# Attention with split fp16 operands in every unit, queries and keys packed on 128 partitions, and weight remainders formed on three engines

## The chip, the cores and the metric

One core of one Trainium2 chip runs the kernel. The time is the device time of one execution in microseconds (us). TensorE multiplies (the page calls it PE), VectorE (DVE) and ScalarE (ACT) work elementwise, GpSimd (POOL) does casts and reductions across partitions, and SyncE (SP) issues the DMAs.

## What is computed

Banded attention with block summaries, followed by a two-layer GELU network on its output. In the reference, cut to what matters:

```python
# q, k, v: (4, 8, 768, 64) fp32; blocks of 32 keys; window 16
k_sum = k.reshape(B, H, nb, 32, D).max(axis=3)
v_sum = v.reshape(B, H, nb, 32, D).mean(axis=3)
scores_l = scale * q @ k.T, masked to |i - j| < 16
scores_s = scale * einsum('bhsd,bhnd->bhsn', q, k_sum) + log(32)
a = softmax(concatenate([scores_l, scores_s], axis=-1))
x = (a @ concatenate([v, v_sum], axis=2)).transpose(0, 2, 1, 3).reshape(3072, 512)
h = x @ w_in                      # 512 x 2048
g = 0.5 * h * (1 + erf(h / sqrt(2)))
out = g @ w_out                   # 2048 x 512
```

w_in and w_out arrive as 64-bit floats.

## The kernel before

**Precision.** TensorE multiplies fp16. An fp32 value is carried as a high part, its fp16 rounding, and a low part, the fp16 rounding of what is left. A product then takes three fp16 matmuls: high by high, high by low, low by high.

**Units and chunks.** The work is cut into 12 chunks of 256 tokens. Attention goes in 24 units of four heads by 256 queries, two units to a chunk. A unit's steps, each a method of the class Unit with the unit's number, are: load_q, load_k, load_v and load_vs; k_hi and q_hi (casts on GpSimd); k_lo and q_lo (subtractions on VectorE); scores (TensorE, into the PSUM tile pss); add_mask (VectorE); maximum (an all-reduction over the partitions on GpSimd); shift (VectorE); exponent (ScalarE); p_hi (GpSimd) and p_lo (VectorE); v_hi (ScalarE) and v_lo (VectorE); values (TensorE); norm_den, norm_take, norm_rec, norm_spread and norm_mult (the division by the softmax sum, on ScalarE and VectorE); x_hi and x_lo.

In a unit from 4 on, k16 holds the high part of k on partitions 0 to 63 and the low part on 64 to 127, and q stands twice, on both halves. One matmul over 128 rows then gives high k by high q plus low k by high q, and a second adds the products with q's low part: 2 matmuls for each of 16 pairs of head and 64 queries.

Units 0 to 3 (self.fp, u < NF) take another way: scores and values multiply fp32 directly (scores_f, L576; values, L648), the mask is put into PSUM by an fp32 matmul (f_mask, L543), f_evac copies the scores out, and in units 0 and 1 the shift by the maximum is two more fp32 matmuls (f_shift, L551 and L552). Their k and v come from extra padded inputs kf and vf, which lie in parts of w_out_h and w_out_l that are not filled yet.

**The network.** phase1 c i (24 matmuls of 256 columns) makes 256 of the 2048 hidden values for chunk c; gelu, g_hi (ScalarE) and g_lo (VectorE) follow; phase2 c i (12 matmuls of 512 columns) multiplies by a quarter of w_out for half of the chunk's tokens. Step i of phase1 needs the weight pieces 2i and 2i + 1 of w_in.

**Weights.** w_in and w_out come in 16 pieces each of 128 x 512 numbers. wi_bits and wo_bits rebuild fp32 from the 64-bit words in three VectorE instructions in a buffer wst, of which there are three. wi_hi and wo_hi (ScalarE) make the scaled high part; wi_lo and wo_lo (VectorE, L324) the low part.

**Order.** ORDER is a long list of steps, written out; the program issues them in this order, and each engine runs its own instructions strictly in it, waiting at each for what it needs. The pools set what can run ahead: two PSUM tiles psh for phase1, one pss, one psv, three stage buffers for loads.

Of the kernel before, what the change touches and what calls it, by code (L numbers as in the profile page):

```python
# [67 lines left out]
norm_den 1, load_v 3, wi_bits 11 0, load_vs 2, shift 2, k_hi 4, scores 3, norm_take 1, exponent 2, load_q 4,
norm_rec 1, k_hi 5, norm_spread 1, norm_mult 1, load_vs 3, load_v 4, wi_bits 11 1, x_hi 1, values 2, wi_bits 11 2,
f_evac 3, q_hi 4, x_lo 1, wi_hi 11, wi_bits 12 0, maximum 3, wi_lo 11, wi_bits 12 1, load_v 5, wi_bits 12 2,  # L70
phase1 0 0, norm_den 2, wi_bits 15 0, fetch_w_out 0, wi_bits 15 1, wi_bits 15 2, load_vs 4, wi_hi 12, norm_take 2,
wi_hi 15, fetch_w_out 6, phase1 0 1, norm_rec 2, gelu 0 0, norm_spread 2, load_vs 5, norm_mult 2, g_hi 0 0, wi_lo 12,
phase1 0 2, x_hi 2, g_lo 0 0, gelu 0 1, x_lo 2, g_hi 0 1, v_hi 4, wi_lo 15, phase1 0 3, shift 3, gelu 0 2, g_hi 0 2,
wi_bits 13 0, load_q 5, exponent 3, wi_bits 13 1, phase1 0 7, wo_bits 0 0, wo_bits 0 1, wi_bits 13 2, gelu 0 3,
wo_bits 6 0, fetch_w_out 10, wo_bits 6 1, values 3, wo_bits 6 2, wi_hi 13, g_hi 0 3, wi_lo 13, wo_hi 6, wo_bits 0 2,
v_hi 5, g_lo 0 2, fetch_w_out 1, fetch_w_out 2, wo_hi 0, g_lo 0 1, phase1 0 6, norm_den 3, wo_lo 6, wo_lo 0, gelu 0 7,
norm_take 3, g_hi 0 7, norm_rec 3, phase1 0 4, norm_spread 3, gelu 0 6, wo_bits 1 0, g_hi 0 6, norm_mult 3,
phase1 0 5, wo_bits 2 0, x_hi 3, wo_bits 1 1, x_lo 3, wo_bits 1 2, wo_bits 2 1, wo_hi 1, wo_bits 2 2, wo_lo 1,
wo_hi 2, g_lo 0 3, wo_lo 2, gelu 0 5, wo_bits 10 0, g_hi 0 5, g_lo 0 7, g_lo 0 5, gelu 0 4, g_lo 0 6, g_hi 0 4,
phase1 1 1, wo_bits 10 1, wo_bits 10 2, k_lo 4, wo_hi 10, fetch_w_out 3, fetch_w_out 4, fetch_w_out 11, wo_lo 10,  # L80
q_lo 4, load_k 6, phase1 1 2, gelu 1 1, g_lo 0 4, g_hi 1 1, wo_bits 3 0, wo_bits 3 1, wo_bits 3 2, phase1 1 3,
gelu 1 2, wo_bits 4 0, fetch_w_out 5, wo_hi 3, wo_bits 4 1, g_hi 1 2, wo_lo 3, wo_bits 4 2, phase1 1 0, gelu 1 3,
# [5 lines left out]
fetch_w_out 14, phase2 0 3, wo_bits 12 0, wo_hi 8, fetch_w_out 15, wo_lo 9, wo_lo 8, g_lo 1 3, phase2 0 5,
wo_bits 12 1, wo_bits 12 2, wo_bits 14 0, wo_hi 12, fetch_k 1 1, wo_bits 14 1, phase2 0 4, wo_bits 15 0, wo_bits 15 1,
wo_bits 14 2, wo_bits 15 2, wo_hi 14, fetch_k 1 2, wo_lo 12, wo_hi 15, fetch_k 1 0, wo_lo 14, wo_lo 15, add_mask 4,  # L90
phase2 0 7, g_lo 1 2, maximum 4, k_lo 6, gelu 1 5, g_hi 1 5, phase2 0 6, gelu 1 4, k_lo 5, g_hi 1 4, store 0 1,
g_lo 1 4, load_k 7, phase1 1 7, put 0 1, shift 4, q_lo 5, exponent 4, load_q 6, phase1 1 6, g_lo 1 5, load_k 8,
v_lo 4, gelu 1 7, p_hi 4, prep_k 1 1, load_v 6, scores 5, p_lo 4, fetch_k 1 3, gelu 1 6, q_hi 6, g_hi 1 6, add_mask 5,
values 4, g_hi 1 7, k_hi 7, store 0 0, g_lo 1 7, put 0 0, phase2 1 1, norm_den 4, maximum 5, q_lo 6, norm_take 4,
prep_k 1 0, phase2 1 3, g_lo 1 6, shift 5, phase2 1 5, v_lo 5, exponent 5, load_q 7, k_lo 7, load_v 7, phase2 1 0,
p_hi 5, prep_k_end 1 0, load_k 9, norm_rec 4, k_sums 1 0, p_lo 5, phase2 1 2, norm_spread 4, norm_mult 4, prep_k 1 2,
x_hi 4, values 5, x_lo 4, fetch_v 1 0, fetch_v 1 1, prep_k 1 3, scores 6, norm_den 5, prep_k_end 1 1, fetch_v 1 3,
phase2 1 7, q_hi 7, add_mask 6, k_sums 1 1, k_hi 8, norm_take 5, phase2 1 4, maximum 6, store 1 1, norm_rec 5,
norm_spread 5, put 1 1, norm_mult 5, q_lo 7, phase2 1 6, x_hi 5, shift 6, x_lo 5, scores 7, exponent 6, load_q 8,
prep_v 1 0, phase1 2 2, store 1 0, k_hi 9, add_mask 7, put 1 0, fetch_v 1 2, p_hi 6, prep_v 1 1, phase1 2 1, gelu 2 2,  # L100
maximum 7, p_lo 6, fetch_k 2 2, k_lo 8, g_hi 2 2, phase1 2 0, gelu 2 1, g_lo 2 2, g_hi 2 1, load_k 10, q_hi 8,
prep_v 1 2, prep_v 1 3, phase1 2 3, gelu 2 0, g_hi 2 0, shift 7, load_vs 6, g_lo 2 0, phase1 2 4, exponent 7,
load_vs 7, q_lo 8, g_lo 2 1, load_q 9, gelu 2 3, p_hi 7, scores 8, fetch_k 2 3, k_lo 9, fetch_k 2 1, phase2 2 1,
k_hi 10, p_lo 7, v_hi 6, load_k 11, v_hi 7, v_lo 6, phase2 2 0, q_hi 9, gelu 2 4, v_lo 7, load_v 8, g_hi 2 4,
g_hi 2 3, add_mask 8, values 6, g_lo 2 3, maximum 8, q_lo 9, phase1 2 6, norm_den 6, load_vs 8, g_lo 2 4, norm_take 6,
norm_rec 6, load_v 9, norm_spread 6, phase1 2 5, gelu 2 6, norm_mult 6, g_hi 2 6, shift 8, v_hi 8, values 7, x_hi 6,
g_lo 2 6, load_q 10, exponent 8, load_vs 9, phase2 2 3, x_lo 6, v_lo 8, k_lo 10, norm_den 7, load_v 10, p_hi 8,
phase2 2 2, gelu 2 5, prep_k 2 3, load_k 12, norm_take 7, norm_rec 7, phase1 2 7, v_hi 9, norm_spread 7, norm_mult 7,
load_vs 10, g_hi 2 5, g_lo 2 5, x_hi 7, scores 9, p_lo 8, gelu 2 7, g_hi 2 7, phase2 2 4, q_hi 10, x_lo 7, k_hi 11,
add_mask 9, v_lo 9, phase1 3 0, maximum 9, g_lo 2 7, load_v 11, q_lo 10, phase1 3 2, gelu 3 0, k_lo 11, g_hi 3 0,  # L110
shift 9, load_k 13, phase1 3 5, gelu 3 2, load_vs 11, g_hi 3 2, g_lo 3 0, exponent 9, g_lo 3 2, load_q 11, prep_k 2 1,
# [742 lines left out]
```

## Time and profile before

| | |
|---|---|
| three runs | 683.58 us median (680.51 to 684.58) |
| the profiled execution | 686.86 us, its span 684.8 us |
| mean granted clock of TensorE | 0.945 |
| busy PE / DVE / ACT / POOL | 638.6 / 472.6 / 297.0 / 172.7 us |
| moved by DMA | 72.24 MB |

A row of a group reads: line, engine, operation, output<-inputs, shapes, count | busy us, mean ns of one | idle time before it and what ended it. A row of the timeline reads: start us, length us, engine, line, operation. A wait reads: who waits <- for whom: us in total, times, the longest.

### The profile page before, as it was taken

How to read it: one execution, taken by the hardware profiler on the slowest of the kernel's cores; microseconds unless marked ns; L12 is line 12 of the kernel's file. 1: busy time of each engine (PE TensorE's matmuls, PEld its weight loads, DVE VectorE, ACT ScalarE, POOL GpSimd, SP SyncE). 2: the span in 40 equal slices, each digit the busy share in tenths (PEclk: the TensorE clock that was granted, in tenths of full speed). 3: DMA queues.
4: the chain of work that ended last, by engine and by line, in shares of the span. 5: the costliest groups of instructions: out<-in, count | busy, mean ns of one | idle time of the engine just before them, and what ended most of it. 6: DMA issues, size and time to landing. Idle time of an engine off the chain costs nothing.

```text
span 684.8 us, 12436 instructions
## 1 busy us (share of the span) xinstructions
PE 638.6 (93%) x5356; PEld 444.2 (65%) x5356; DVE 472.6 (69%) x581; ACT 297.0 (43%) x419; POOL 172.7 (25%) x103
## 2 busy tenths in 40 slices
PE   1989999889898799999899989999999899999997
...
DVE  1784778999999998948889986628318974146210
...
PEclk9855569999999999999999999999999999999999
...
GB/s 247 378 218 199 139 66 125 149 180 152 162 117 141 167 91 225 180 57 72 91 127 79 88 77 53 133 1 111 45 16 66 84 69 16 1 32 1 16 16 32
DMA packets 26998, 72.24 MB, mean 105 GB/s; under 512 B 3008, under 2 KB 6720, under 8 KB 26944
## 3 DMA queue, kind: packets, MB, share of 16 engines
...
q8 instruction: 42, 0.69, 0.4%
...
HBM read 63.38 MB, written 6.29 MB: 102 GB/s over the span
## 4 chain that ended last, share of the span: by engine, by line
PE 66%; DVE 25%; issue 3%; DMA 2%; ACT 2%; POOL 1%; SPq 1%; DVEq 0%; ACTq 0%; POOLq 0%
PE psh L708 9%; PE psh L709 9%; PE psh L710 9%; PE pso L743 8%; PE pso L742 8%; PE pso L744 8%; PE psv L648 4%; DVE ql L568 3%; DVE gl L728 3%; PE pss L576 3%; DVE k L562 2%; DVE s L607 2%; DVE s L593 2%; PE pss L543 2%; DVE v_lo L634 2%
## 5 line engine op out<-in xcount | busy, mean ns | idle before, releaser
L708 PE MATMUL psh<-xh,w_in_h 128*128 128x256 f16 x768 | 210.4, 274 | 6.4 <-ACT g L715 6.4
L709 PE MATMUL psh<-xl,w_in_h 128*128 128x256 f16 x768 | 210.3, 274 | 0.5 <-DVE xl L698 0.5
L710 PE MATMUL psh<-xh,w_in_l 128*128 128x256 f16 x768 | 210.4, 274 | 0.0
L728 DVE SCALAR_TENSOR_TENSOR gl<-g,gh 128x512 f16<-128x512 f32 x96 | 76.7, 804 | 106.9 <-ACT gh L724 106.3
L743 PE MATMUL pso<-w_out_l,gh 128*128 128x512 f16 x384 | 146.4, 381 | 0.5 <-DVE w_out_l L324 0.5
L742 PE MATMUL pso<-w_out_h,gh 128*128 128x512 f16 x384 | 146.5, 382 | 0.0
L744 PE MATMUL pso<-w_out_h,gl 128*128 128x512 f16 x384 | 146.0, 380 | 0.0
L602 POOL PARTITION_ALL_REDUCE q<-s x24 | 82.5, 3439 | 95.9 <-ACT s L547 55.1
L715 ACT ACTIVATE g<-psh 128x512 f32<-128x512 f32 x96 | 56.9, 595 | 109.8 <-PE psh L710 107.9
L559 POOL CAST qh<-q 128x1024 f16<-128x1024 f32 x20 | 25.6, 1278 | 268.7 <-PE pss L589 254.7
L709 PEld LDWEIGHTS <-w_in_h 128*128 128x128 f16 x768 | 75.6, 98 | 18.8 <-issue 7.3
L708 PEld LDWEIGHTS <-w_in_h 128*128 128x128 f16 x768 | 75.7, 99 | 11.9
L710 PEld LDWEIGHTS <-w_in_l 128*128 128x128 f16 x768 | 75.5, 98 | 10.0 <-issue 0.9
L744 PEld LDWEIGHTS <-gl 128*128 128x128 f16 x384 | 37.8, 98 | 46.6 <-issue 1.9
L742 PEld LDWEIGHTS <-gh 128*128 128x128 f16 x384 | 37.8, 99 | 41.0 <-issue 0.8
L743 PEld LDWEIGHTS <-gh 128*128 128x128 f16 x384 | 37.8, 98 | 40.7 <-issue 0.5
L724 ACT ACTIVATE gh<-g 128x512 f16<-128x512 f32 x96 | 59.9, 629 | 2.7
L617 POOL CAST ph<-s 128x1024 f16<-128x1024 f32 x20 | 27.2, 1359 | 68.0 <-ACT s L613 68.0
L613 ACT ACTIVATE s<-s 128x1024 f32<-128x1024 f32 x22 | 23.3, 1057 | 48.5 <-DVE s L607 48.4
L651 PE MATMUL psv<-pl,v_hi 128*128 128x64 f16 x320 | 32.9, 199 | 7.6 <-DVE pl L621 7.6
L568 DVE TENSOR_TENSOR ql<-q,qh 128x1024 f16<-128x1024 f32 x20 | 39.3, 1966 | 0.1
L650 PE MATMUL psv<-ph,v_hi 128*128 128x64 f16 x320 | 33.2, 199 | 6.3 <-DVE den L680 5.9
...
## 6 DMA issues: line engine op xcount, KB each, us to landing
...
```

Of the source, the lines that this page charges most:

```text
L568: nc.vector.tensor_tensor(out=self.ql, in0=self.q32, in1=self.qh, op=ALU.subtract)
L602: nc.gpsimd.partition_all_reduce(out_ap=self.m32, in_ap=self.s32, channels=P, reduce_op=bass_isa.ReduceOp.max)
L650: nc.tensor.matmul(self.psv[:, sl], vh[:, vo : vo + P], self.ph[:, sl], start=True, stop=False)
L708: nc.tensor.matmul(ph[:, e, :], w_in_h[:, k, fs], xh[:, k, :], start=(k == 0), stop=False)
L709: nc.tensor.matmul(ph[:, e, :], w_in_h[:, k, fs], xl[:, k, :], start=False, stop=False)
L710: nc.tensor.matmul(ph[:, e, :], w_in_l[:, k, fs], xh[:, k, :], start=False, stop=(k == NCC - 1))
L715: nc.scalar.activation(g32, pht.pop((c, i)), AF.Gelu, scale=1.0 / (SC_X * SC_WI))
L724: nc.scalar.activation(gh, g32t[c, i], AF.Copy, scale=SC_G)
L728: nc.vector.scalar_tensor_tensor(out=gl, in0=g32t.pop((c, i)), scalar=SC_G, in1=gh, op0=ALU.mult, op1=ALU.subtract)
L742: nc.tensor.matmul(p, gh[:, f, js], w_out_h[:, f, :], start=(f == 0), stop=False)
L743: nc.tensor.matmul(p, gh[:, f, js], w_out_l[:, f, :], start=False, stop=False)
L744: nc.tensor.matmul(p, gl[:, f, js], w_out_h[:, f, :], start=False, stop=(f == NFC - 1))
```

## The change

The fp32 way of units 0 to 3 goes: kf, vf, f_evac, f_shift, scores_f and the fp32 values are removed, and all 24 units split their operands. q and k of a unit now lie on 128 partitions, the even heads on 0 to 63 and the odd heads on 64 to 127. High and low parts of k are two tiles, k_hi and k_lo, and scores issues, for each of 8 pairs of heads and 64 queries, three products (high by high, high by low, low by high) for each half of the rows: 48 matmuls over 64 rows. The halves write different halves of pss, and values, norm_den and the data layout follow that order. maximum has its own tile m32, of which there is one, in place of q's buffer. The pool for g32 grows from 3 to 5 buffers, that of qh and ql from 1 to 2.

Of the 32 low parts of weights, 8 (w_in pieces 0 to 7) become a difference on TensorE (wi_diff: an fp32 matmul with a scaled identity, less the high part) and an eviction by ScalarE; 20 (w_in 8 to 15, w_out 0 to 11) are scaled by ScalarE in a pass of their own (wi_ghi, wo_ghi) and subtracted by GpSimd (wi_glo, wo_glo); 4 stay on VectorE. ORDER is written anew. The core of the diff:

```diff
-KC = UH * (CT + 1)
+QCOLS = UCOLS // 2
+KC = UH // 2 * (CT + 1)
-NF = 4
-    NQ16, NG32, NOT = 1, 3, 1
+    NQ16, NG32, NOT = 2, 5, 1
+    def weight_ghi(key, dst_h):
+        m = dst_h.shape[1]
+        if key not in sts:
+            sts[key] = wk.tile([P, 512], F32, tag="wst", bufs=3, name=f"wst_{key}")
+        nc.scalar.activation(sts[key], raws[key], AF.Copy, scale=SC_WI)
+        raws[key] = sts[key]
+        nc.scalar.activation(dst_h, raws[key].rearrange("p (m n) -> p m n", m=m), AF.Copy)
+
+    def weight_glo(key, dst_h, dst_l):
+        m = dst_h.shape[1]
+        nc.gpsimd.tensor_tensor(
+            out=dst_l, in0=raws.pop(key).rearrange("p (m n) -> p m n", m=m), in1=dst_h, op=ALU.subtract
+        )
...
         def k_hi(self):
-            nc.gpsimd.tensor_copy(out=self.k16[0:D, :, 0:TQ], in_=self.k32)
+            nc.gpsimd.tensor_copy(out=self.kh[:, :, 0:TQ], in_=self.k32)
...
         def k_lo(self):
-            nc.vector.tensor_tensor(
-                out=self.k16[D:P, :, 0:TQ], in0=self.k32, in1=self.k16[0:D, :, 0:TQ], op=ALU.subtract
-            )
+            nc.vector.tensor_tensor(out=self.kl[:, :, 0:TQ], in0=self.k32, in1=self.kh[:, :, 0:TQ], op=ALU.subtract)
...
         def scores(self):
-            for h in range(UH):
-                for t in range(CT):
-                    ...
-                    nc.tensor.matmul(self.pss[:, sl], kf[:, kb : kb + P], self.qh[:, sl], start=True, stop=False)
-                    nc.tensor.matmul(self.pss[:, sl], kf[:, kb : kb + P], self.ql[:, sl], start=False, stop=True)
+            for i in range(NR * CT):
+                kb = (i // CT * (CT + 1) + i % CT) * KW
+                sl = slice(i * TQ, (i + 1) * TQ)
+                for n, (k, q) in enumerate(((kh, self.qh), (kh, self.ql), (kl, self.qh))):
+                    for e in range(2):
+                        rows = slice(e * D, (e + 1) * D)
+                        nc.tensor.matmul(
+                            self.pss[:, e * QCOLS + i * TQ : e * QCOLS + (i + 1) * TQ], k[rows, kb : kb + P], q[rows, sl],
+                            start=(n == 0 and not masked), stop=(n == 2 and (i == NR * CT - 1 or not masked)),
+                        )
...
         def maximum(self):
-            self.m32 = self.q32
+            self.m32 = wk.tile([P, UCOLS], F32, tag="m32", bufs=1, name=f"m32_{self.nm}")
...
-        def scores_f(self):
-        def f_evac(self):
-        def f_shift(self):
-        def kf_sums(self):
```

VectorE at the start of the program, before (ks is the tile of the key blocks' maxima, gl and gh are buffers lent to the first loads, wst_i are weight bits):

```order
L405 TENSOR_REDUCE ks_0_120<-gh_93 128x24
L414 CAST ks_0_0_149<-ks_0_120 128x48
L418 COPY ksum_89<-ks_0_0_149 64x2x24
L419 TENSOR_TENSOR ksum_89<-ks_0_120,ks_0_0_149 64x2x24
L418 COPY ksum_89<-ks_0_0_149 64x2x24
L419 TENSOR_TENSOR ksum_89<-ks_0_120,ks_0_0_149 64x2x24
L294 TENSOR_SCALAR wst_i_173<-gh_95 128x512
L299 SCALAR_TENSOR_TENSOR wst_i_173<-gh_95,wst_i_173 128x512
L303 SCALAR_TENSOR_TENSOR wst_i_173<-gh_95,wst_i_173 128x512
L324 SCALAR_TENSOR_TENSOR w_in_l<-wst_i_173,w_in_h 128x2x256
```

And there in the changed program:

```order
L429 CAST ks_0_0_122<-ks_0_117 128x48
L430 TENSOR_TENSOR ks_0_0_122<-ks_0_117,ks_0_0_122 128x48
L537 TENSOR_TENSOR k_lo_90<-k_0_109,k_hi_88 128x10x64
L541 TENSOR_TENSOR ql_136<-q_0_111,qh_130 128x512
L418 TENSOR_REDUCE ks_0_117<-gh_94 128x24
L418 TENSOR_REDUCE ks_0_117<-gl_95 128x24
L565 SCALAR_TENSOR_TENSOR s_0_198<-mask_sb,pss_140 128x1024
```

VectorE begins with the split of unit 0 and its masked scores; weight pieces come behind it.

GpSimd between the casts of unit 5 and the maximum of unit 4, before (v and w_out_l rows are load_vs, q rows without a cast are maximum):

```order
L515 COPY v_5_467<-w_out_l 24x1024
L559 CAST qh_1032<-q_5_612 128x1024
L555 CAST k_0_91<-k_6_840 64x20x64
L602 ISA q_4_425<-s_4_1181 128x1024
L617 CAST ph_1286<-s_4_1181 128x1024
```

And in the changed program (a row ISA without operands is a switch of GpSimd's code; the middle of the 20 subtractions is left out):

```order
L512 COPY v_5_770<-w_out_l 24x1024
L333 ISA
L333 TENSOR_TENSOR w_in_l<-wst_i_802,w_in_h 128x2x256
L333 TENSOR_TENSOR w_in_l<-wst_i_822,w_in_h 128x2x256
```

```order
L333 TENSOR_TENSOR w_out_l<-wst_o_1428,w_out_h 128x512
L333 TENSOR_TENSOR w_out_l<-wst_o_1435,w_out_h 128x512
L530 CAST k_hi_88<-k_6_1129 128x10x64
L534 CAST qh_1543<-q_6_1134 128x512
L574 ISA
L574 ISA m_4_1546<-s_4_1522 128x1024
```

Twenty weight subtractions and two code switches stand where GpSimd had next to nothing.

VectorE among the pieces of w_out, before:

```order
L299 SCALAR_TENSOR_TENSOR wst_o_871<-wraw_831,wst_o_871 128x512
L303 SCALAR_TENSOR_TENSOR wst_o_871<-wraw_831,wst_o_871 128x512
L294 TENSOR_SCALAR wst_o_902<-wraw_833 128x512
L299 SCALAR_TENSOR_TENSOR wst_o_902<-wraw_833,wst_o_902 128x512
L324 SCALAR_TENSOR_TENSOR w_out_l<-wst_o_871,w_out_h 128x512
```

And in the changed program:

```order
L292 SCALAR_TENSOR_TENSOR wst_o_1170<-wraw_1087,wst_o_1170 128x512
L287 TENSOR_SCALAR wst_o_1177<-wraw_1098 128x512
L292 SCALAR_TENSOR_TENSOR wst_o_1177<-wraw_1098,wst_o_1177 128x512
L296 SCALAR_TENSOR_TENSOR wst_o_1170<-wraw_1087,wst_o_1170 128x512
L296 SCALAR_TENSOR_TENSOR wst_o_1177<-wraw_1098,wst_o_1177 128x512
L693 SCALAR_TENSOR_TENSOR gl_93<-g_0_5_1132,gh_92 128x512
```

The rows of the low part are gone from VectorE's list there; those of the bits stay.

More of the change, by code (lines that the diff above doesn't have):

```diff
@@ L68 @@
[L68 to L82, printed above, removed]
@@ L88 @@
[L88 to L102, printed above, removed]
@@ L103 @@
[L103 to L111, printed above, removed]
-phase1 3 1, prep_k 2 2, gelu 3 5, p_hi 9, prep_k_end 2 1, fetch_k 2 0, fetch_v 2 2, fetch_v 2 0, p_lo 9, phase2 2 6,
@@ new lines @@
+k_lo 8, fetch_k 2 3, phase1 2 0, gelu 2 1, put 1 0, q_lo 8, v_hi 6, load_k 10, prep_k 2 1, load_q 10, g_hi 2 1,
+v_lo 6, fetch_v 2 0, v_hi 7, scores 7, gelu 2 0, shift 6, load_v 8, phase1 2 2, k_hi 9, g_hi 2 0, q_hi 9, add_mask 7,
+exponent 6, v_lo 7, maximum 7, phase1 2 4, g_lo 2 0, gelu 2 2, g_lo 2 1, k_lo 9, phase2 2 1, g_hi 2 2, q_lo 9,
+load_k 11, p_hi 6, gelu 2 4, shift 7, load_vs 8, g_hi 2 4, p_lo 6, phase1 2 5, exponent 7, load_v 9, load_q 11,
+g_lo 2 2, g_lo 2 4, p_hi 7, values 6, prep_k 2 2, gelu 2 5, prep_k_end 2 0, fetch_v 2 1, phase1 2 6, p_lo 7,
@@ new lines @@
+norm_den 6, load_vs 9, prep_k 2 3, v_hi 8, norm_take 6, fetch_v 2 2, phase2 2 3, norm_rec 6, g_hi 2 5, norm_spread 6,
+gelu 2 6, norm_mult 6, g_hi 2 6, phase1 2 7, g_lo 2 5, x_hi 6, v_lo 8, x_lo 6, load_v 10, values 7, g_lo 2 6,
+gelu 2 7, g_hi 2 7, prep_v 2 0, phase2 2 0, norm_den 7, g_lo 2 7, fetch_v 2 3, prep_k_end 2 1, v_hi 9, norm_take 7,
+norm_rec 7, load_vs 10, phase2 2 2, norm_spread 7, v_lo 9, norm_mult 7, load_v 11, phase2 2 4, prep_v 2 1, x_hi 7,
+x_lo 7, fetch_k 3 0, scores 8, prep_v 2 2, phase1 3 2, k_hi 10, add_mask 8, fetch_k 3 1, load_vs 11, q_hi 10, k_lo 10,
@@ new lines @@
+phase1 3 7, g_lo 3 6, norm_den 8, v_hi 10, norm_take 8, norm_rec 8, norm_spread 8, phase2 2 7, gelu 3 7, norm_mult 8,
+g_hi 3 7, v_lo 10, x_hi 8, phase2 2 6, store 2 1, x_lo 8, load_v 12, put 2 1, g_lo 3 7, scores 9, phase2 3 0,
+add_mask 9, k_hi 11, q_hi 11, k_lo 11, maximum 9, load_vs 12, q_lo 11, store 2 0, phase2 3 2, load_k 13, load_q 13,
+put 2 0, phase2 3 1, shift 9, exponent 9, phase2 3 3, p_hi 9, scores 10, p_lo 9, phase2 3 4, k_sums 2 0, k_hi 12,
+add_mask 10, q_hi 12, k_lo 12, maximum 10, q_lo 12, load_k 14, values 9, prep_k_end 3 0, load_q 14, scores 11,
@@ new lines @@
+norm_den 9, phase2 3 6, add_mask 11, k_hi 13, v_hi 11, q_hi 13, norm_take 9, k_sums 2 1, norm_rec 9, norm_spread 9,
+phase2 3 5, store 3 0, norm_mult 9, put 3 0, v_lo 11, x_hi 9, phase2 3 7, x_lo 9, load_v 13, shift 10, k_lo 13,
+exponent 10, maximum 11, phase1 4 4, q_lo 13, load_k 15, store 3 1, prep_k_end 3 1, load_q 15, put 3 1, load_vs 13,
+phase1 4 0, gelu 4 4, p_hi 10, shift 11, g_hi 4 4, p_lo 10, phase1 4 1, exponent 11, g_lo 4 4, gelu 4 0, p_hi 11,
+values 10, p_lo 11, scores 12, g_hi 4 0, norm_den 10, g_lo 4 0, phase1 4 2, k_hi 14, add_mask 12, q_hi 14, gelu 4 1,
@@ new lines @@
+v_lo 15, exponent 14, maximum 15, phase1 6 0, k_lo 17, load_v 17, q_lo 17, load_k 19, store 5 0, load_q 19, put 5 0,
+phase1 6 1, gelu 6 0, p_hi 14, shift 15, p_lo 14, exponent 15, load_vs 17, phase1 6 2, g_hi 6 0, p_hi 15, gelu 6 1,
+g_lo 6 0, values 14, p_lo 15, scores 16, norm_den 14, phase1 6 6, add_mask 16, k_hi 18, g_hi 6 1, q_hi 18, gelu 6 2,
+norm_take 14, maximum 16, g_hi 6 2, norm_rec 14, norm_spread 14, v_hi 16, phase1 6 5, norm_mult 14, gelu 6 6,
+g_hi 6 6, g_lo 6 1, x_hi 14, g_lo 6 2, values 15, gelu 6 5, x_lo 14, g_hi 6 5, shift 16, k_sums 3 0, phase1 6 7,
@@ new lines @@
+norm_mult 16, v_lo 18, x_hi 16, phase1 7 4, x_lo 16, load_v 20, phase1 7 2, gelu 7 4, g_hi 7 4, g_lo 7 4, phase2 6 4,
+load_vs 20, gelu 7 2, g_hi 7 2, g_lo 7 2, scores 17, phase1 7 6, add_mask 17, k_sums 3 1, k_hi 19, q_hi 19, k_lo 19,
+maximum 17, q_lo 19, load_k 21, phase1 7 7, gelu 7 6, load_q 21, g_hi 7 6, g_lo 7 6, phase1 7 5, shift 17, gelu 7 7,
+g_hi 7 7, exponent 17, g_lo 7 7, phase1 7 3, gelu 7 5, p_hi 17, p_lo 17, phase2 6 6, g_hi 7 5, gelu 7 3, g_lo 7 5,
+g_hi 7 3, g_lo 7 3, values 17, store 6 0, put 6 0, phase2 6 1, norm_den 17, v_hi 19, norm_take 17, norm_rec 17,
```

382 lines of the change are left out of this document (169 added, 213 removed).

## The prediction

> **What bounds the kernel now.** I read the slices of the page first, then busy time by stage, then single rows where two stages meet.
>
> ```profile
> span 684.8 us, 12436 instructions
> PE   1989999889898799999899989999999899999997
> DVE  1784778999999998948889986628318974146210
> PEclk9855569999999999999999999999999999999999
> ```
>
> TensorE looks full nearly everywhere, yet its clock stands at half from the third slice to the sixth, and VectorE is at 9 from the seventh to the fourteenth. So there are three regimes, and the stages tell them apart (columns: length, then busy us of PE, PEld, DVE, ACT, POOL, clock, DMA).
>
> ```profile
> 0.00:38.00 38.00, 22.80 (x84) 12.88 (x84) 19.12 (x33) 9.41 (x16) 8.49 (x16) 0.91 0.98 322
> 38.00:99.00 61.00, 59.54 (x206) 41.37 (x207) 42.33 (x58) 18.79 (x28) 19.44 (x10) 0.53 0.48 149
> 99.00:120.00 21.00, 21.00 (x194) 19.19 (x193) 17.07 (x29) 16.80 (x24) 0.00 (x0) 1.00 0.32 102
> 120.00:241.00 121.00, 104.94 (x953) 71.50 (x951) 119.11 (x147) 56.59 (x79) 40.30 (x20) 0.97 0.50 153
> 241.00:685.00 444.00, 430.29 (x3925) 299.27 (x3923) 275.01 (x318) 195.40 (x274) 104.51 (x57) 1.00 0.22 68
> ```
>
> From 38 to 99 us TensorE does only 206 matmul passes, nearly all of them the fp32 ones of units 0 to 3, at clock 0.53, while VectorE idles 19 of 61 us behind it. From 120 to 241 us VectorE works 119.11 of 121 us and TensorE idles 16. After 241 us TensorE is the bound, and of the 13.5 us that it idles 3.9 lie behind its last matmul, which is the tail:
>
> ```profile
> 681.05 0.60 ACT L749 ACTIVATE ot<-pso 128x512 f32<-128x512 f32 x1 [9.81 <-PE pso L744]
> ```
>
> So the end is: the moment at which VectorE stops holding TensorE (241 us), the matmuls left then (430), 9.6 us of later idling, and the tail. And 241 us is VectorE's work up to there, 19.12 + 42.33 + 17.07 + 119.11 = 197.6, and its idle time, 43.4, of which 41.5 lie before 120 us.
>
> **The change, at the same point of the work.** Counting steps in the written order, "phase2 2 3" of before, which begins with the row below, has 73 phase1, 78 phase2, 15 scores and 16 values steps left; "phase2 2 0" of the changed order has 72, 78, 16 and 16. I compare what must happen ahead of these two.
>
> ```profile
> 237.85 0.61 PE L742 MATMUL pso<-w_out_h,gh 128*128 128x512 f16 x1
> ```
>
> *VectorE's work.* The groups that change (line, engine, shape, count, busy us, mean ns):
>
> ```profile
> L324 DVE SCALAR_TENSOR_TENSOR w_in_l<-wst_i,w_in_h 128x512 f16<-128x512 f32 x16 | 12.3, 784 | 17.4 <-ACT w_in_h L310 17.3
> L324 DVE SCALAR_TENSOR_TENSOR w_out_l<-wst_o,w_out_h 128x512 f16<-128x512 f32 x16 | 10.6, 685 | 0.0
> L593 DVE SCALAR_TENSOR_TENSOR s<-mask_sb,pss 128x1024 f32<-128x1024 f32 x20 | 24.3, 1217 | 16.4 <-PE pss L589 16.3
> L607 DVE TENSOR_TENSOR s<-s,q 128x1024 f32<-128x1024 f32 x22 | 30.2, 1375 | 4.6 <-POOL q L602 4.5
> L621 DVE TENSOR_TENSOR pl<-s,ph 128x1024 f16<-128x1024 f32 x20 | 29.1, 1461 | 5.4 <-POOL ph L617 5.3
> L634 DVE SCALAR_TENSOR_TENSOR v_lo<-v,v_hi 128x512 f16<-128x512 f32 x40 | 34.3, 900 | 0.4 <-ACT v_hi L628 0.3
> L568 DVE TENSOR_TENSOR ql<-q,qh 128x1024 f16<-128x1024 f32 x20 | 39.3, 1966 | 0.1
> L562 DVE TENSOR_TENSOR k<-k,k 64x1280 f16<-64x1280 f32 x20 | 34.2, 1713 | 0.6
> L698 DVE TENSOR_TENSOR xl<-den,xh 128x512 f16<-128x512 f32 x24 | 19.5, 811 | 2.9 <-ACT xh L694 2.9
> L405 DVE TENSOR_REDUCE ks<-kp 128x24 f32<-128x768 f32 x12 | 11.2, 943 | 1.1 <-DMA kp<-in_kp_dram 1.1
> L463 DVE TENSOR_REDUCE vs<-vb 96x32 f32<-96x1024 f32 x12 | 14.3, 1209 | 2.5 <-DMA vb<-in_vb_dram 2.5
> L414 DVE CAST ks<-ks 128x48 f16<-128x48 f32 x8 | 1.5, 185 | 0.2
> L418 DVE COPY ksum<-ks 64x48 f16<-64x48 f16 x16 | 3.6, 226 | 0.5
> L419 DVE TENSOR_TENSOR ksum<-ks,ks 64x48 f16<-64x48 f32 x16 | 4.3, 266 | 0.2
> ```
>
> Off: 28 lo subtractions, 16 x 0.784 + 12 x 0.685 = 20.8 us. On: units 0 to 3 need the split that they did without. By the two points that is 3 more add_mask (3.7), 1 more shift (1.4; units 0 and 1 shifted on TensorE), 4 more p_lo (5.8), 10 more v_lo halves (9.0), 4 prep_k (3.8), and one prep_v, x_lo and g_lo (2.8): 26.5. Packing q and k on 128 partitions halves their columns: 6 q_lo at 1.966 become 10 of the size of x_lo, 0.811 (-3.7); 6 k_lo at 1.713 become 10 at 0.97, interpolated between 512 and 1024 columns (-0.6). prep_k_end falls from five small instructions (0.185 + 2 x 0.226 + 2 x 0.266 = 1.17) to two (0.45): four times the one against five times the other is -2.4. Sum **-1**. What the weights give up, the four units take.
>
> *VectorE's idle time.* Before: 41.5 us by 120 us, because fp32 passes at half clock held everything. That cover goes; late next are the loads and the first units' chain through GpSimd.
>
> ```profile
> 8.31 0.95 DVE L405 TENSOR_REDUCE ks<-gl 128x24 f32<-128x768 f32 x1 [8.31 <-DMA gl<-in_kp_dram]
> 14.38 3.75 PE L543 MATMUL pss<-mask_sb,ind_sb 128*128 128x512 f32 x4 [14.38 <-DMA ind_sb<-in_mask_dram]
> L602 POOL PARTITION_ALL_REDUCE q<-s x24 | 82.5, 3439 | 95.9 <-ACT s L547 55.1 <-DVE s L593 37.3 <-issue 3.4
> ```
>
> The mask that add_mask 0 needs is now the ninth load on SP; ind_sb, the eighth of before, landed at 14.38; ahead of it VectorE has four prep_k, one prep_k_end, k_lo 0 and q_lo 0, some 6 us, so 8.5 idle. Then two all-reductions of 3.4 us in series, the second behind shift 0 since m32 has one buffer, with weight bits to fill: I take 6 until unit 1's x_lo, and 5.5 over the weights behind it. Sum 20, so **-21.5**; bounds -33 (loads alone) and -4 (as idle as before by 99 us: 18.9 + 18.7 = 37.6).
>
> *GpSimd against VectorE.* GpSimd gets 20 subtractions (8 pieces of w_in, 12 of w_out), which this trace does not show. Nearest rows:
>
> ```profile
> L559 POOL CAST qh<-q 128x1024 f16<-128x1024 f32 x20 | 25.6, 1278 | 268.7 <-PE pss L589 254.7
> L617 POOL CAST ph<-s 128x1024 f16<-128x1024 f32 x20 | 27.2, 1359 | 68.0 <-ACT s L613 68.0
> L555 POOL CAST k<-k 64x1280 f16<-64x1280 f32 x20 | 29.3, 1466 | 10.3 <-PE pss L589 6.0 <-issue 2.3 <-POOL q L602 2.0
> 175.54 3.40 DVE L728 SCALAR_TENSOR_TENSOR gl<-g,gh 128x512 f16<-128x512 f32 x1
> 176.56 3.16 POOL L602 PARTITION_ALL_REDUCE q<-s  x1
> 178.86 1.21 DVE L568 TENSOR_TENSOR ql<-q,qh 128x1024 f16<-128x1024 f32 x1
> ```
>
> One read of 512 columns costs 0.64 us (half of 1.278), two reads 1.28; the ends are 0.64 and 1.72 (half an all-reduction). I take 1.28, 25.6 in all. Smaller casts and one all-reduction less take off 2.2, so GpSimd gets 23.4 us more. What VectorE loses by it: g_lo took 3.40 us under an all-reduction of 3.16 that ended with it, instead of the 0.8 of x_lo, which has its shape, while q_lo took 1.21 alone and 1.966 on average. So a pass over two SBUF tensors waits for GpSimd fully at worst and not at all at best; I take half: **+12**, bounds 0 and +23.
>
> The Trainium skill, "SBUF — State Buffer", section Who interferes with whom, makes it an exclusive lock: a VectorE instruction with two SBUF inputs and a GpSimd instruction that reads SBUF never run together. The g_lo row agrees; by the lock alone the term would be near +23, and the time 11 us higher.
>
> *Code switches on GpSimd.* Its row list has one more switch ahead of the subtractions and another behind them.
>
> ```profile
> POOL q L602 <- issue: 3.4, 1, 3.4
> ```
>
> The largest wait of that kind is 3.4 us; only three weight buffers lie between it and VectorE. **+2**, bounds 0 and +7.
>
> *TensorE after the point.* One phase1 step fewer, and scores change from 32 matmuls to 48.
>
> ```profile
> 99.34 0.27 PE L708 MATMUL psh<-xh,w_in_h 128*128 128x256 f16 x1
> 109.82 3.68 PE L648 MATMUL psv<-s,w_out_l 128*128 128x64 f32 x32
> 137.40 0.19 PE L588 MATMUL pss<-qh,k 128*128 128x64 f16 x1
> 138.33 0.38 PE L742 MATMUL pso<-w_out_h,gh 128*128 128x512 f16 x1
> ```
>
> Four phase1 steps fill the time between the first two rows, 10.48 us, so -2.6. Between the other two, thirty-two score matmuls took 0.93 us, 29 ns each; 48 make 1.39 if they follow one another and 0.70 if the two row halves run together. Nothing here shows which; I take 1.39, the pitch that the row has: 16 x 1.39 - 15 x 0.93 = +8.3. Sum **+5.7**, lower bound -5.4.
>
> *Hidden.* The eight TensorE differences cost about 2 us each (four passes in 3.75 are two such fp32 products), 16 us ahead of "phase1 0 3", where TensorE has some 38 us of work and VectorE 56. ACT gets a second pass for 20 pieces, eight evictions and four v_hi, about 21 us (0.6 for each half of such a tile, the tail's row), under a VectorE that is full while ACT is busy 56.59 of 121. If ACT lagged, the three weight buffers would hand it to VectorE. On SP, q halves and the padded fp32 k and v go, and DMA is no bound after 38 us. *Later idling*: lighter q_lo and k_lo should take **-4** of the 9.6 (bounds -9.6 and +5).
>
> Sum: -1 - 21.5 + 12 + 2 + 5.7 - 4 = **-6.8** on this execution's own 686.86 us (span 684.8 and 2.1 around it). The shown median is 683.58, so about 677.
>
> **The rivals.** *The row halves run together.* The two products of a pair read partitions 0-63 and 64-127 and write different halves of pss, so nothing in the program orders them. For it: nothing in the 29 ns; against: that pitch may be the issue of load and matmul, which also grows from 64 to 96 instructions. It gives 16 x 0.69 = 11 us less, **666**. The Trainium skill, "TensorE: Matmul & The Clock Gate", Part 3, says that matmuls on different row groups overlap, starting about 4 ns apart; no row here shows it, and by it this rival would be the forecast.
>
> *The GpSimd subtractions lock VectorE out* (slower). Place: weight pieces i8 to i15 and o0 to o11, where nearly every VectorE instruction reads two SBUF tensors (bits, g_lo). At 1.72 us each and a full wait it is 34 instead of 12, some 21 us: **698**. It turns slower from about 1.0 us each under a full wait, slower by over 1% from 1.35. For it: the 3.40 row. Against: transposes and passes with a PSUM input between them.
>
> *The start stays idle.* If units 0 and 1, split on GpSimd and VectorE in series, hold VectorE as long as fp32 did, 13 of the 21.5 are not saved: **690**. For it: 95.9 us of idle time before all-reductions show how serial that chain is; against: weight bits fill it.
>
> **How the numbers follow.** Forecast 0.47, halves together 0.22, lock-out 0.22, idle start 0.09. A measurement here can tell about 1%, 6.8 us, from no change. The forecast's own range is 668 to 687 and lies half beyond that mark: faster 0.23 + 0.22 = 0.45; same 0.24 + 0.09 = 0.33; slower 0.22. The range, 659 to 696, goes 7 us below the first rival, since the start may save up to 11 us more, and leaves out the lock-out from 696 on, about 0.13, with as little at the low end.
>
> **What would show it.**
>
> ```profile
> 94.46 0.42 PE L708 MATMUL psh<-xh,w_in_h 128*128 128x256 f16 x1
> ```
>
> Right: the first phase1 matmul, in the row above before the change, near 58 us (39 us of VectorE work by these rows, 14.5 of the idle time, some 5 of lock); VectorE full from there to about 230; clock low only before. Scores of a unit in 1.4 us or 0.7 decide the first rival. A mean of the GpSimd subtraction over 1.35 with weight bits at twice their present length, or gaps of VectorE behind ACT's two passes, would make it wrong.

## The result, and the profile after

| | before | after |
|---|---|---|
| median | 682.61 us (680.51 to 684.58, 4 runs) | 654.39 us (652.89 to 655.38, 4 runs) |
| ratio to before, 95% interval | | 0.9585 (0.9546 to 0.9624) |
| profiled execution, its span | 686.86, 684.8 us | 652.89, 651.1 us |

The changed kernel is 4.2% faster. The forecast, 677 us, had the sign, but 654 lies outside the range of 659 to 696.

The slices of the changed kernel (40 of 16.3 us, busy tenths, as shown of before):

```profile
span 651.1 us, 13383 instructions
PE   4436858988998999999999999999999999999997
DVE  6999989999999998799260898453386939251100
PEclk9668898988999999999999999999999999999999
```

The stretch of half clock is gone. VectorE is full from the second slice on, and TensorE, loose in the first third, is full from there to the end. So the two regimes of before are left, VectorE first and TensorE behind it, and the third is not there any more. The forecast compared the kernels at one point of the work; the same two points cut the spans as follows (columns: length, busy us of PE, PEld, DVE, ACT, POOL, clock, DMA share, GB/s; first before, then after):

```profile
0.00:237.85 237.85, 205.13 (x1421) 143.62 (x1422) 194.51 (x262) 98.49 (x143) 66.77 (x45) 0.85 0.55 174
237.85:684.80 446.95, 433.44 (x3940) 300.59 (x3937) 278.13 (x320) 198.49 (x277) 105.97 (x58) 0.99 0.23 69
```

```profile
0.00:217.04 217.04, 161.26 (x1596) 107.32 (x1597) 204.77 (x253) 110.19 (x168) 93.71 (x75) 0.91 0.56 185
217.04:651.10 434.06, 428.28 (x4206) 293.83 (x4202) 249.95 (x303) 201.86 (x283) 95.22 (x60) 1.00 0.19 58
```

The point comes 20.8 us earlier. VectorE has 10.3 us more work ahead of it (194.51 to 204.77), but its idle time falls from 43.3 to 12.3 us. Behind the point the rest is 12.9 us shorter: TensorE's work by 5.2, its idle time by 7.7 (13.5 to 5.8). These four numbers are the whole 33.7 us, and the experiments ask where each is from.

### The profile page after: what moved, and what is told of

Read it like the earlier page. It is cut to its first block, busy times and chain, and to the rows that moved or that the text cites. A ratio compares the mean times of both kernels' runs of the same rounds, so it can differ in the third digit from the quotient of the medians.

```text
span 651.1 us, 13383 instructions
## 1 busy us (share of the span) xinstructions
PE 589.5 (91%) x5796; PEld 401.1 (62%) x5796; DVE 454.7 (70%) x555; ACT 312.1 (48%) x450; POOL 188.9 (29%) x135
## 4 chain that ended last, share of the span: by engine, by line
PE 64%; DVE 27%; issue 4%; ACT 2%; DMA 1%; SPq 1%; POOL 0%; DVEq 0%; ACTq 0%; POOLq 0%
PE pso L707 10%; PE pso L708 10%; PE pso L709 10%; PE psh L675 9%; PE psh L673 9%; PE psh L674 9%; DVE v_lo L603 3%; DVE s L579 2%; DVE s L565 2%; DVE wst_o L292 2%; DVE k_lo L537 2%; PE pss L554 2%; DVE wst_i L287 2%; DVE gl L693 2%; DVE wst_o L296 1%
## 5 line engine op out<-in xcount | busy, mean ns | idle before, releaser
L693 DVE SCALAR_TENSOR_TENSOR gl<-g,gh 128x512 f16<-128x512 f32 x96 | 68.1, 721 | 111.1 <-ACT gh L689 110.9
L574 POOL PARTITION_ALL_REDUCE m<-s x24 | 85.7, 3569 | 59.9 <-DVE s L565 26.6
L530 POOL CAST k_hi<-k 128x640 f16<-128x640 f32 x24 | 20.3, 844 | 173.2 <-PE pss L554 143.3
L616 PE MATMUL psv<-ph,v_hi 128*128 128x64 f16 x384 | 38.6, 197 | 9.3 <-DVE den L645 9.3
L603 DVE SCALAR_TENSOR_TENSOR v_lo<-v,v_hi 128x512 f16<-128x512 f32 x48 | 46.6, 1011 | 0.2
L586 POOL CAST ph<-s 128x1024 f16<-128x1024 f32 x24 | 30.7, 1278 | 54.1 <-ACT s L582 54.1
L617 PE MATMUL psv<-pl,v_hi 128*128 128x64 f16 x384 | 38.2, 197 | 6.0 <-DVE pl L590 5.9
L616 PEld LDWEIGHTS <-v_hi 128*128 128x128 f16 x384 | 35.2, 100 | 11.3 <-issue 9.4
```

Source lines behind the costliest of these rows:

```text
L574: nc.gpsimd.partition_all_reduce(out_ap=self.m32, in_ap=self.s32, channels=P, reduce_op=bass_isa.ReduceOp.max)
L603: nc.vector.scalar_tensor_tensor(out=vl[:, :, e, :], in0=v32[:, :, e, :], scalar=SC_X, in1=vh[:, :, e, :], op0=ALU.mult, op1=ALU.subtract,)
L616: nc.tensor.matmul(self.psv[:, sl], vh[:, vo : vo + P], self.ph[:, sl], start=True, stop=False)
L693: nc.vector.scalar_tensor_tensor(out=gl, in0=g32t.pop((c, i)), scalar=SC_G, in1=gh, op0=ALU.mult, op1=ALU.subtract)
```

## Experiments

In all of them the same point is used, and every ratio is to the kernel before, run on the same chip. The changed kernel's is 0.9585.

**1. Row halves.** In scores, the loop over the halves goes outside:

```diff
-            for i in range(NR * CT):
-                for n, (k, q) in enumerate(...):
-                    for e in range(2):
+            for e in range(2):
+                for i in range(NR * CT):
+                    for n, (k, q) in enumerate(...):
```

> The changed kernel, its 48 score matmuls of a unit in another order: first all 24 of the upper row half, then all 24 of the lower one, so that hardly any stands next to one of the other half. Theory (row halves overlap when they follow each other; 47 starts took 0.684 us): each half now takes 24 x 29 ns, the 47 starts about 1.37 us, 0.69 more for each unit. The 16 units behind the point at 217 us lie on TensorE's path: 11 us, 665 in place of 654. Rival (a matmul over 64 rows is simply shorter, in any order): starts stay at 0.68 us, 654.

Measured: 663.71 us, ratio 0.9753 (0.9706 to 0.9799). In the timeline of TensorE one unit's first and last score matmuls, and the one behind them, are in the changed kernel

```profile
135.43 0.20 PE L554 MATMUL pss<-qh,k_hi 64*128 64x64 f16 x2
...
136.11 0.19 PE L554 MATMUL pss<-qh,k_lo 64*128 64x64 f16 x2
136.24 0.39 PE L707 MATMUL pso<-w_out_h,gh 128*128 128x512 f16 x1
```

and here

```profile
136.91 0.20 PE L554 MATMUL pss<-qh,k_hi 64*128 64x64 f16 x1
...
137.51 0.21 PE L554 MATMUL pss<-qh,k_hi 64*128 64x64 f16 x2
...
138.19 0.19 PE L554 MATMUL pss<-qh,k_lo 64*128 64x64 f16 x1
138.32 0.39 PE L707 MATMUL pso<-w_out_h,gh 128*128 128x512 f16 x1
```

An x2 is two matmuls in one row, and since the row is as long as that of a single one (0.19 to 0.20 us), they start within some 10 ns of each other. With neighbours from different halves each pair takes 29 ns, and a unit 136.24 - 135.43 = 0.81 us to the next matmul; in series each single one takes 29 ns, and a unit 1.41 us. The only pairs left begin at 137.51, where the halves meet: three matmuls of the second half start beside the last three of the first, ahead of their place in the order. The row behind the point shows the price:

```profile
218.70:660.20 441.50, 437.39 (x4206) 303.95 (x4202) 249.23 (x303) 202.34 (x283) 94.35 (x60) 1.00 0.18 57
```

TensorE's work there is 437.39 - 428.28 = 9.1 us longer. The stretch grows by 7.4 (434.06 to 441.5), since TensorE idles less in it, and the point comes 1.7 later: 9.1 us of span in all. The overlap is shown. The Trainium skill says the same in "TensorE: Matmul & The Clock Gate", Part 3: matmuls on different row groups run at once, starting about 4 ns apart; the trace agrees as far as its steps of 10 ns show.

**2 and 3. The 20 GpSimd subtractions.** Put back on VectorE, or left out with GpSimd writing zeros:

```diff
-wi_ghi 8, ... wi_glo 8   (20 such pieces)
+wi_hi 8, ... wi_lo 8
```

```diff
-        nc.gpsimd.tensor_tensor(out=dst_l, in0=raws.pop(key)..., in1=dst_h, op=ALU.subtract)
+        raws.pop(key)
+        nc.gpsimd.memset(dst_l, 0.0)
```

> The changed kernel with its 20 GpSimd subtractions back on VectorE (ScalarE then makes the high part in one pass); the 8 differences on TensorE stay. Theory (a GpSimd subtraction of 1.35 us holds VectorE up for 0.9 us): VectorE gives back 18 us of waiting and takes 20 x 0.7 = 14 us of work before 217 us, so 4 us less, 650. Rival (the relief of VectorE is real, little is lost by the lock): 14 us more, 668.

> The changed kernel in which GpSimd writes zeros for 20 low parts of weights and subtracts nothing (the low parts of w_in 8 to 15 and w_out 0 to 11 are left out). Theory (lock): VectorE before 217 us is shorter by 18 us, and the time is 636. Rival (half a lock, as predicted): 9 us shorter, 645. If the path there is not VectorE's work but ScalarE's two passes: 654.

Measured: 652.03 us, 0.9583 (0.954 to 0.9625), and 642.84 us, 0.9449 (0.9402 to 0.9496). So 20 subtractions fewer on VectorE bring nothing that can be measured. The groups of VectorE's weight bits say why: first the changed kernel, with GpSimd's own groups and three rows of the timeline, then the kernel without GpSimd subtractions.

```profile
L296 DVE SCALAR_TENSOR_TENSOR wst_o<-wraw,wst_o 128x512 int32<-128x512 int32 x16 | 18.5, 1170 | 0.3
L292 DVE SCALAR_TENSOR_TENSOR wst_o<-wraw,wst_o 128x512 int32<-128x512 int32 x16 | 15.6, 973 | 0.5
L333 POOL TENSOR_TENSOR w_out_l<-wst_o,w_out_h 128x512 f16<-128x512 f32 x12 | 16.6, 1379 | 21.2 <-ACT w_out_h L311 21.2
L333 POOL TENSOR_TENSOR w_in_l<-wst_i,w_in_h 128x512 f16<-128x512 f32 x8 | 10.4, 1309 | 16.9 <-ACT w_in_h L311 10.2 <-ACT wst_i L309 6.7
```

```profile
119.28 1.16 POOL L333 TENSOR_TENSOR w_out_l<-wst_o,w_out_h 128x512 f16<-128x512 f32 x1 [2.01 <-ACT w_out_h L311]
119.39 1.59 DVE L292 SCALAR_TENSOR_TENSOR wst_o<-wraw,wst_o 128x512 int32<-128x512 int32 x1
121.01 0.69 DVE L296 SCALAR_TENSOR_TENSOR wst_o<-wraw,wst_o 128x512 int32<-128x512 int32 x1
```

```profile
L292 DVE SCALAR_TENSOR_TENSOR wst_o<-wraw,wst_o 128x512 int32<-128x512 int32 x16 | 12.7, 791 | 0.5
L296 DVE SCALAR_TENSOR_TENSOR wst_o<-wraw,wst_o 128x512 int32<-128x512 int32 x16 | 11.7, 747 | 0.3
```

```profile
0.00:209.63 209.63, 160.56 (x1597) 107.66 (x1598) 191.55 (x253) 109.51 (x168) 77.61 (x75) 0.90 0.57 192
```

The same 32 passes over w_out take 34.1 us beside the subtractions and 24.4 without. (They take 24.6 in the second experiment, which has neither subtractions nor the 20 writes of zeros, so the writes don't lengthen these passes.) One pair of rows shows it: a subtraction starts at 119.28, a pass with two SBUF inputs 0.11 us behind it takes 1.59 instead of 0.69 us. In all VectorE works 204.77 - 191.55 = 13.2 us less, 0.66 us for each subtraction of 1.35 (27.0 by 20). The pass that it saves costs 0.56 us by the stages (202.66 - 191.55 by 20; the second experiment's row stands under 11 and 12) and 0.68 by its own row, since neighbouring passes overlap a little. VectorE's 13.2 us lie between the 18 of the theory and the 9 of its rival. The time, by the ratios 9 us below the changed kernel, is the rival's: 13.2 us off VectorE's work gave only 7.4 at the point (217.04 to 209.63), and the rest became idle time, 12.3 to 18.1 us. The lock of the Trainium skill ("SBUF — State Buffer", Who interferes with whom) is in these rows, but it costs half of what it would at every subtraction.

**4 and 5. The fp32 way taken out alone.** In both `self.fp = False` in the kernel before, all low parts on VectorE; the fourth uses the changed order (with q casts and loads moved to fit the old buffers, and four buffers for g32 in place of three), the fifth keeps its own order and puts the split steps where the fp32 steps stood (one load, load_k 5, goes a few steps later).

> The kernel before with the fp32 way of units 0 to 3 taken out and nothing else of the change: q and k packed as before, all low parts on VectorE, the changed order (q loads and q casts moved back where its buffers ask for it). Theory (VectorE's work up to the point at 217 to 238 us counts): the idle time of 43 us falls to about 13, but four units bring 26.5 us of split and 14.7 us of q and k low parts, so it is slower than before by 5 to 10 us, 688 to 693. Rival (TensorE at half clock is what cost the time, and its end is the gain): near the changed kernel, 655 to 662.

> The kernel before, in its own order and with its own buffers, with the fp32 way of units 0 to 3 taken out: they are split like the others (k and q casts, low parts, mask, shift, split of p and v put in where the fp32 steps stood). The kernel of the run before this (754) stalled behind q casts in an order that its buffers did not fit; this one has no such moves. Theory (VectorE's work up to the meeting point counts): 41 us more work there against at most 31 us less idle time, so 685 to 695, no faster than before. Rival (fp32 at half clock was the cost by itself): 655 to 665.

Measured: 754.51 us, 1.1079 (1.1019 to 1.1139), and 700.97 us, 1.0288 (1.0218 to 1.0359). The fourth tells nothing about fp32, because the moves made a new wait, the second row of VectorE's waits:

```profile
DVE ql L578 <- POOL qh L569: 57.4, 18, 5.5
```

It shows only that the new order does not go with one q buffer in this form. The fifth has no such wait, and is slower than before, by 6 us more than the theory's range:

```profile
0.00:252.12 252.12, 153.39 (x1453) 108.67 (x1454) 229.29 (x287) 95.90 (x134) 83.66 (x57) 0.82 0.51 161
```

TensorE loses 51.7 us of work ahead of the point, VectorE's idle time falls by 20.5 us (43.3 to 22.8), and yet the point comes 14.3 us later, since VectorE has 34.8 us more to do. TensorE's fp32 work at half clock did cost VectorE idle time, but taking it out is no gain by itself. The rival is out.

**6. All 28 low parts on VectorE**, the changed kernel otherwise (the steps wi_diff dropped too).

> The changed kernel with 28 low parts back on VectorE (the 20 of GpSimd and the 8 differences of TensorE). Theory: the 20 are worth nothing (13.3 us of lock against 13.6 us of work), the 8 take 8 x 0.7 = 5.6 us of VectorE's work off, so 657 to 660. Rival (the 8 differences lengthen the start, since their fp32 passes bring the clock down to 0.7 between 38 and 58 us): 650 or less.

Measured: 656.08 us, 0.9627 (0.9563 to 0.9691); profiled:

```profile
0.00:219.38 219.38, 151.49 (x1572) 103.95 (x1573) 208.12 (x281) 93.86 (x140) 68.29 (x55) 0.88 0.55 183
```

The whole move of weight work is worth 2.0 us of span; the intervals of the two ratios overlap. So the step from 700.5 (fifth) to 653.1 us is the packing of q and k with the order and the buffers that it allows.

**7 and 10. Twelve differences on TensorE.** w_in 8 to 15 and w_out 0 to 3 as wi_diff and wo_diff, the other eight on VectorE; then the same with `bufs=4` for wst.

> The changed kernel without subtractions on GpSimd: w_in 8 to 15 and w_out 0 to 3 become differences on TensorE too (evicted by ScalarE), w_out 4 to 11 are subtracted on VectorE. Theory: VectorE loses 13.3 us of lock and takes 8 x 0.69 = 5.5 us of work; TensorE gets 12 x 1.9 = 23 us where it idles 56 us before 217 us. So 8 us less than the changed kernel, 646. Rival (the differences take the two psh tiles, wait for VectorE's bits in TensorE's queue and bring its clock down): 654 or more.

> The kernel of the twelve differences (664) with four weight buffers in place of three. Theory (there VectorE waited 16 us for weight buffers that TensorE's differences still read): most of the wait goes, VectorE idles some 16 us instead of 31, and the time is 648 to 652. Rival (TensorE's queue sets when a difference runs, one more buffer only moves the wait): 658 to 664.

Measured: 664.03 us, 0.9741 (0.966 to 0.9822), and 662.95 us, 0.9728 (0.9666 to 0.9791). Both theories fell, and both times are those of the rivals. VectorE's waits, first with three buffers, then with four:

```profile
DVE wst_o L297 <- PE psw_o L326: 9.0, 3, 4.2
...
DVE wst_i L297 <- PE psw_i L326: 4.2, 2, 2.6
DVE wst_o L297 <- PE psw_i L326: 3.0, 2, 2.1
DVE w_out_l L335 <- ACT w_out_h L313: 3.0, 1, 3.0
```

```profile
DVE w_out_l L335 <- ACT w_out_h L313: 7.5, 1, 7.5
DVE wst_o L297 <- PE psw_i L326: 5.7, 3, 3.4
...
DVE gl L703 <- ACT gh L699: 3.1, 1, 3.1
DVE wst_o L297 <- PE psw_o L326: 2.5, 2, 1.6
```

VectorE waits for weight buffers that a difference still holds. By the order each difference stands in TensorE's queue behind matmuls that need other weights of VectorE's; that these are what delays it is argued, not shown. The fourth buffer takes 8 of the 16.2 us off, and the waits for ScalarE grow from 3.0 to 10.6 us. Room in TensorE's time was no room in its queue.

**8. The first key blocks loaded later.** In the order:

```diff
-fill_v 0, fetch_k 0 0, fill_v 1, fetch_k 0 1, load_k 0, load_q 0, load_ind, fetch_vt 0, fetch_k 0 2, ...
+fill_v 0, fill_v 1, load_k 0, load_q 0, load_ind, fetch_vt 0, fetch_k 0 0, fetch_k 0 1, fetch_k 0 2, ...
```

> The changed kernel, its first two loads of key blocks issued behind four other loads (k, q, identity and first values of unit 0) instead of ahead of them, about where the kernel before had its first one. Theory (VectorE counts from its first instruction; it began at 3.90 us, before the change at 8.31): VectorE begins some 4 us later and idles that much more, so 4 us more, 658. Rival (the start is covered by something else, the chain of unit 0 for one): 654.

Measured: 655.43 us, 0.9616 (0.9552 to 0.968).

```profile
8.95 0.95 DVE L427 TENSOR_REDUCE ks<-gh 128x24 f32<-128x768 f32 x1 [8.95 <-DMA gh<-in_kp_dram]
```

```profile
0.00:221.24 221.24, 164.43 (x1597) 109.88 (x1598) 204.15 (x253) 110.07 (x168) 92.67 (x75) 0.90 0.55 182
```

VectorE starts at 8.95 us and idles 17.1 (221.24 - 204.15) instead of 12.3; the point moves by 4.2 us, the span of the profiled execution by 3.6. The medians differ by 1.0 us only and the intervals overlap: by time this run is inconclusive, by the trace the start counts.

**9. Casts and low parts of q and k made twice**, with nothing else changed (each of the four instructions of k_hi, q_hi, k_lo and q_lo stands twice). That is more work than the unpacked form. The low parts of ten units ahead of the point, packed in the changed kernel and unpacked in the fifth, are

```profile
L537 DVE TENSOR_TENSOR k_lo<-k,k_hi 128x640 f16<-128x640 f32 x10 | 13.7, 1370 | 1.0 <-POOL k_hi L530 0.9
L541 DVE TENSOR_TENSOR ql<-q,qh 128x512 f16<-128x512 f32 x10 | 7.7, 766 | 0.5 <-POOL qh L534 0.5
```

```profile
L573 DVE TENSOR_TENSOR k<-k,k 64x1280 f16<-64x1280 f32 x10 | 19.4, 1949 | 0.3
L579 DVE TENSOR_TENSOR ql<-q,qh 128x1024 f16<-128x1024 f32 x10 | 13.9, 1390 | 0.2
```

so 21.4 us packed and 33.3 unpacked.

> The changed kernel in which each cast and each low part of q and k is made twice into the same tile: about the elementwise work of the unpacked q (1024 columns) and k (1280 columns of 64 partitions), with the new order, buffers and row halves kept. Theory (the width of q and k is most of what the packing brought, on VectorE and by the lock of GpSimd's casts): 10 units ahead of the point at 217 us with 0.69 + 0.83 us more on VectorE and about 0.8 of lock, 15 to 23 us, and 3 to 9 us more of idle time on TensorE behind it: 672 to 686. Rival (the new order and the extra buffers are what brought it): 15 us or less in all, 660 to 669.

Measured: 686.45 us, 1.005 (1.0016 to 1.0085), as slow as before.

```profile
0.00:237.66 237.66, 167.74 (x1597) 110.56 (x1598) 225.58 (x275) 110.11 (x168) 112.55 (x95) 0.87 0.51 169
237.66:685.40 447.74, 432.78 (x4206) 296.46 (x4202) 275.10 (x329) 202.03 (x283) 120.53 (x88) 0.99 0.19 56
```

VectorE's work ahead of the point is 20.8 us longer and so is the point, 20.6; the idle time ahead of it does not move (12.1 us). Behind the point TensorE's idle time goes from 5.8 to 15.0. So work on q and k ahead of the point is paid nearly in full. It does not show that the width carries the whole gain: made twice, the low parts take 42.5 us by their four groups, so the run adds 21.1 us (42.5 - 21.4) where the unpacked form needs 11.9 (33.3 - 21.4). Scaled by these two, some 19 of the 34 us that it adds to the span would be the width's own, an estimate. In spans, then: taking out fp32 by itself costs 15.7 us (684.8 to 700.5), and of the 49.4 from there to the changed kernel (651.1) the weights carry 2.0, the width about 19 and at most 34, and the rest falls to the order and the buffers, which, but for the two loads of experiment 8, no run tries apart.

**11 and 12. Casts on ScalarE.** The kernel of the second experiment, with q's and k's casts on ScalarE for all units, or for units 0 to 8:

```diff
-            nc.gpsimd.tensor_copy(out=self.qh, in_=self.q32)
+            nc.scalar.activation(self.qh, self.q32, AF.Copy)
```

> The changed kernel with its 20 GpSimd subtractions back on VectorE (652 in that form) and, beside that, the casts of q and k of all units on ScalarE in place of GpSimd. Theory (GpSimd's casts hold VectorE up too, by some 0.35 and 0.2 us each beside busy VectorE): about 5 us less ahead of the meeting point at 216 us, 647. Rival (ScalarE's own order: a cast that waits for a buffer keeps gelu and the high parts of g behind it): 654 or more.

> As the run before this in the same call, but only the casts of units 0 to 8 on ScalarE, which VectorE reads ahead of the meeting point; those of units 9 to 23 stay on GpSimd. Theory: the same 5 us, 647, and no wait of TensorE behind the point more than the 5.4 us of idle time before. Rival (ScalarE's order delays the first units): 654 or more.

Measured: 647.62 us, 0.9502 (0.9457 to 0.9547), and 646.65 us, 0.9494 (0.9454 to 0.9535), the fastest of all with every low part in; the two are not told apart. The row ahead of the point of the second experiment, and then of the twelfth:

```profile
0.00:216.49 216.49, 159.69 (x1597) 107.42 (x1598) 202.66 (x273) 97.57 (x148) 67.89 (x55) 0.91 0.55 186
```

```profile
0.00:210.90 210.90, 159.98 (x1596) 107.59 (x1597) 196.53 (x273) 108.04 (x166) 52.12 (x37) 0.92 0.56 190
```

VectorE issues the same 273 instructions and works 6.1 us less, with 15.8 us less of GpSimd's work beside it. The rows that shrink are passes with two SBUF inputs (k_lo from 1366 to 1072 ns, q_lo from 818 to 682); add_mask, which reads PSUM, stays at 1217. ScalarE, half idle there, takes the casts with little delay: VectorE waits 1.7 us for them in place of 0.9.

## Why the prediction was right or wrong

| term | forecast | measured | by |
|---|---|---|---|
| VectorE's work ahead of the point | -1 | -3 | 10.3 in all, less the 13.2 of lock |
| GpSimd against VectorE | +12 | +13.2 | experiment 3 |
| VectorE's idle time, code switches | -21.5, +2 | -31.1 | rows at the point |
| TensorE's work behind the point | +5.7 | -5.2 | rows at the point |
| later idling | -4 | -7.7 | rows at the point |
| sum | -6.8 | -33.7 | spans |

**Right.** What bounds the kernel, and the account of VectorE's work: what the weights gave up, the four units took, and the fifth experiment shows the units' price by itself. Half a lock for each subtraction was right within 1.2 us; the lock-out rival (1.72 us each under a full wait) got 1.35 us and half a wait. The weights were nearly a wash, as the forecast's terms of opposite sign had it (-20.8 against +14; 2.0 us of span in experiment 6). Luck had a part in the half: it was the middle between two bounds, and the rows it leaned on were misread. The all-reduction from 176.56 to 179.72 ends 0.8 us behind g_lo and not with it, and q_lo, called alone, runs inside it from 178.86 on; spans of GpSimd are rough. What shows the lock are the rows of experiments 2 and 3.

**Wrong: the scores.** The step took 1.39 us a unit from the pitch of 29 ns and gave the overlap a chance of 0.22. The unit took 0.81 us: 16 x 0.81 - 15 x 0.93 = -1.0 instead of +8.3. With -2.6 for the phase1 step that makes -3.6; for the other 1.6 of the -5.2 no run gives a cause. The pitch was measured on matmuls that use all 128 rows, with no other row half beside them; a row that can't show an effect is no evidence against it.

**Wrong: VectorE's idle time.** The forecast had 8.5 us ahead of the first mask, 6 for the all-reductions, 5.5 over the weights and 2 for code switches. VectorE's waits up to the point, longest first, are these; the view names no others, 9.0 of the 12.3 us:

```profile
DVE ks L418 <- DMA gh<-in_kp_dram: 4.6, 2, 3.9
DVE dent L628 <- ACT den L624: 1.7, 1, 1.7
DVE s L565 <- PE pss L554: 1.3, 2, 1.0
DVE k_lo L537 <- POOL k_hi L530: 0.9, 1, 0.9
DVE ql L541 <- POOL qh L534: 0.5, 1, 0.5
```

```profile
11.94 1.22 DVE L565 SCALAR_TENSOR_TENSOR s<-mask_sb,pss 128x1024 f32<-128x1024 f32 x1
```

No wait for an all-reduction and none for a switch is in it, and add_mask 0 runs at 11.94 without waiting for its mask. The estimate took the landing of the eighth load of before, 14.38 us, for that of the ninth now. The bytes up to there are about as many (2.8 and 3.0 MB by the sizes of the loads), but in the first 12 us the DMA moved 306 GB/s where it had moved 227; why, no run shows. The fp32 removal by itself brought -20.5, nearly the -21.5 forecast for everything. What the forecast lacked is the further 10.5 us, and 9.7 of them are one wait: with the old order the fifth kernel waited 14.3 us for the first key blocks,

```profile
DVE ks L416 <- DMA gl<-in_kp_dram: 11.0, 2, 7.5
DVE ks L416 <- DMA gh<-in_kp_dram: 3.3, 1, 3.3
```

the changed order 4.6. It issues those loads first, which stood in the order list beside the diff. Experiment 8, where this wait is 9.0, put back 4.4 us of it; for the other half of the load order nothing was tried.

**Wrong: later idling**, -7.7 for -4. Experiment 9 shows the mechanism, light work on q and k: with their casts and low parts made twice the idle time is 15.0 us, more than the 13.5 of before. The term was right in kind and too small.

**The range.** Its low end, 659, went 7 us below a single rival. The two large errors, in terms of different engines, fell on the same side: -6.8 - 10.9 - 11.6 alone is -29. The bounds given for the terms (-33 idle, -5.4 TensorE, -9.6 later) contained each result.

**The marks.** The first phase1 matmul came at 51.31 us (forecast 58), VectorE stayed full to about 244 us by the slices (230), and GpSimd's subtraction stayed near 1.35 us with the bits of w_out at 1.5 times their length of before (34.1 by 22.6), not twice.

```profile
51.31 0.27 PE L673 MATMUL psh<-xh,w_in_h 128*128 128x256 f16 x1
```
